# The channel layer in blocks of 512 tokens that run across batches, with its second product turned round

## The chip, the core and the metric

The kernel runs on one core of one Trainium2 chip. A core has a matrix engine (TensorE, PE in the profile, with its weight loads shown apart as PEld), a vector engine (VectorE, DVE), a scalar engine (ScalarE, ACT), a general engine (GpSimd, POOL) and a sync engine (SP) that mainly issues transfers. Each engine takes its instructions in the order in which the program lists them, and semaphores order the engines among each other. SBUF is the working memory and PSUM the memory that matmuls accumulate into; both have 128 partitions. The metric is the device time of one execution in microseconds; lower is better.

## What is computed

The program is a chain of three models on 4 batches of 768 tokens: a recurrent attention, a gated layer, and a token-and-channel mixer. The change touches only the last layer of the mixer, the channel layer. In the reference it is the last two lines of this function (B=4, 768 tokens, 384 features, 1536 hidden features):

```python
def _moe2_ref(x, w_tok1, w_tok2, w_ch1, w_ch2):
    xt = x.transpose(0, 2, 1)
    h = np.maximum(xt @ w_tok1, 0.0) @ w_tok2
    u = x + h.transpose(0, 2, 1)
    h2 = np.maximum(u @ w_ch1, 0.0) @ w_ch2
    return u + h2
```

## The kernel before

**Numbers.** A float32 value that goes into a matmul is split in two values of a shorter format: `hi`, and `lo`, which is the value less `hi`. A product of two such pairs is three matmuls into one sum (`mm3`, L521 to L524): hi by hi, hi by lo, lo by hi. So a line L522, L523 or L524 in the profile is one of those three, whatever layer it belongs to; the layer is read from the tile names behind the arrow. The first operand of `nc.tensor.matmul` behind the output is the one that is held in the array (loaded by a weight load of 128x128), and the second is streamed through it; its columns are the columns of the output.

**The channel layer.** `chan(b,hf,need)` (L632) handles half a batch, 384 tokens, at a time, so there are 8 calls. `L.UT` holds the features of one batch by its 768 tokens, as hi and lo, in the buffer GU. For each of 12 chunks f of 128 hidden features:

- the first product (L638 to L640) gives a tile of 128 hidden features by 384 tokens: 3 chunks of input features, three matmuls each, so 9 matmuls of 384 columns; the weights C1 (in the buffer SB) are held, UT streams
- `evR` (L612) takes the result out of PSUM: ACT makes `hh`, the positive part (L613), and DVE makes `hlo`, what is left of it (L614)
- one chunk later, the second product (L646, L647): for each of 3 groups of 128 tokens, `hh` and `hlo` are held and the weights C2A (buffer VHt) or, for chunks 8 to 11, C2B (buffer SW) stream with 384 output features. That makes 9 more matmuls of 384 columns, into three accumulators `acc` that stay in PSUM over all 12 chunks.

At the end three DVE additions put the accumulators onto the input `xn` (L651), which has tokens on partitions like them, and three transfers of 192 KB on SP's queue write the result (L652).

**Transposes.** Before the first call for a batch, `trans(b,L.UT)` (L541) turns the whole batch round: 18 TensorE transposes of 128x128 (L546), three to a PSUM bank, and six evictions `evT` (L538, L539), each an ACT copy to hi and a DVE subtraction to lo. No other PE work is listed between them and the matmuls around them.

**Order of the work around it.** The Python generators write out the order. `bank()` hands out five PSUM banks in turn, and three more are the accumulators. `push` emits an eviction right behind its matmuls. While the layer starts, its weights are still being read and converted: `chl` (L707) is a generator of steps, each of which loads 128x256 pieces of 64-bit input (L434), rebuilds float32 on DVE (L446 to L451) and splits it, hi on ACT (L422) and lo on POOL (L423). `both(a,b,n)` (L665) advances it by n steps for each `yield` of the layer (`n[0]`, `n[1]`, `n[2]` are 0.5, 0.2 and 0.7), and `need(k)` forces as many steps as a chunk needs before it can be emitted. The layer before, `tok2` (L626), ends with additions onto `xn` (L601).

Of the kernel before, what the change touches and what calls it, by code (L numbers as in the profile page):

```python
# [6 lines left out]
F32=mybir.dt.float32; F32R=mybir.dt.float32r; I32=mybir.dt.int32; I64=mybir.dt.int64; BF16=mybir.dt.bfloat16  # L7
# [404 lines left out]
def _dense(tc,I,O,xn,cfg):  # L412

    nc=cfg.get('wrap',lambda x:x)(tc.nc)
    THR=2.0**(0x70-127)*1.125
    A0=1.0/0.044715; CG=0.7978845608028654*0.044715
    me=_Dense(); es=ExitStack(); esT=ExitStack(); esS=ExitStack()
    R=lambda t:t.bitcast(F32)
    def split(src,hi,lo,w,p=False):

        if p: nc.gpsimd.tensor_copy(hi,src)
        else: nc.scalar.copy(hi,src)  # L422
        (nc.gpsimd if w else nc.vector).tensor_tensor(lo,src,R(hi),ALU.subtract)  # L423
    def load(src,hi,lo,parts,step=256,pool=None,ahead=2,g=1,out=None,lag=1):
# [30 lines left out]
        for i in range(0,n+lag*g,g):  # L455
            for j in range(max(i-lag*g,0),min(i-lag*g+g,n)):
                r=slice(todo[j][1],todo[j][1]+step)
                if out is None: split(Fs[j],hi[:,r],lo[:,r],True)
                else:
                    w=[pool.tile([128,step],F32R,name=n_,bufs=2) for n_ in ('sh','sl')]  # L460
                    split(Fs[j],w[0],w[1],True,True)
                    for x,y in zip(out(r),w): nc.gpsimd.dma_start(x,R(y))
            if i<n:
# [7 lines left out]
    def start(scr):  # L471
# [3 lines left out]
        psB=[es.enter_context(tc.tile_pool(name="psD",bufs=2,space=PS,side="right"))]  # L475
# [3 lines left out]
        idt=PW.tile([128,128],F32,name="idt")  # L479
# [12 lines left out]
        def bank():  # L492
            nb[0]+=1
            return psB[order[0][nb[0]%len(order[0])]].tile([128,512],F32,name="ps")

        hl=lambda t,o,n:(t[:,o:o+n],t[:,o+n:o+2*n])
# [4 lines left out]
        C2A=[a.rearrange("p (f e) -> p f e",e=384) for a in hl(VHt,0,3072)]  # L501
        XT=[X[:,i] for i in range(2)]
        XN=[X[:,i].rearrange("p k t -> p (k t)").rearrange("p (s e) -> p s e",e=384) for i in range(2)]
        L=_Dense()
# [11 lines left out]
        def late2():  # L516
            GU=es.enter_context(tc.tile_pool(name="pg",bufs=1)).tile([128,6144],F32R,name="GU")
            L.GT=[a.rearrange("p (d t) -> p d t",t=768) for a in hl(GU,0,3072)]
            L.UT=[a.rearrange("p (k t) -> p k t",t=768) for a in hl(GU,0,2304)]
            L.H1=[a.rearrange("p (k e) -> p k e",e=384) for a in hl(GU,4608,768)]  # L520
        def mm3(ps,L,Rr,first,last):  # L521
            nc.tensor.matmul(ps,L[0],Rr[0],start=first,stop=False)  # L522
            nc.tensor.matmul(ps,L[0],Rr[1],start=False,stop=False)  # L523
            nc.tensor.matmul(ps,L[1],Rr[0],start=False,stop=last)  # L524
# [4 lines left out]
        def push(it):  # L529

            few=len(order[0])==2
            if few: tick()
            more=next(it,0)!=0
            if not few: tick()
            if more: live.append(it)
        def drain():
            while live: tick()
        def evT(ps,hi,lo):  # L538
            nc.scalar.copy(hi,ps); nc.vector.tensor_tensor(lo,ps,R(hi),ALU.subtract)  # L539
            yield 1  # L540
        def trans(b,dst):  # L541
            for k in range(3):
                for hf in range(2):
                    ps=bank()[:,0:384]
                    for i in range(3):
                        nc.tensor.transpose(ps[:,128*i:128*i+128],xn[b][:,3*hf+i,128*k:128*k+128],idt)  # L546
                    push(evT(ps,dst[0][:,k,384*hf:384*hf+384],dst[1][:,k,384*hf:384*hf+384]))
                    yield 1
# [51 lines left out]
        def evX(ps,b,s):  # L600
            nc.vector.tensor_tensor(xn[b][:,s],xn[b][:,s],ps,ALU.add)  # L601
            yield 1
# [9 lines left out]
        def evR(ps,hi,lo):  # L612
            nc.scalar.activation(hi,ps,AF.Relu)  # L613
            nc.vector.scalar_tensor_tensor(lo,ps,0.0,R(hi),op0=ALU.max,op1=ALU.subtract)  # L614
            yield 1
# [10 lines left out]
        def tok2(b):  # L626
            for s in range(6):
# [1 line left out]
                for k in range(2):  # L629
                    mm3(ps,[w[:,k,128*s:128*s+128] for w in TK2],[h[:,k,:] for h in L.H1],k==0,k==1)  # L630
                push(evX(ps,b,s)); yield 1
        def chan(b,hf,need):  # L632
            acc=[psB[2].tile([128,512],F32,name="ps")[:,:384] for _ in range(3)]
            hd=[None]*12
            for f in range(13):
                if f<12:
                    need(2*(f//4)+1)
                    ps=bank()[:,:384]  # L638
                    for k in range(3):
                        mm3(ps,[w[:,k,128*f:128*f+128] for w in L.C1],[x[:,k,384*hf:384*hf+384] for x in L.UT],k==0,k==2)  # L640
                    hi=ph[0].tile([128,384],F32R,name="hh"); lo=ph[0].tile([128,384],F32R,name="hlo")
                    push(evR(ps,hi,lo)); hd[f]=(hi,lo)
                    yield 1
                if f>0:
                    need(2*((f-1)//4)+2)
                    for i in range(3):  # L646
                        mm3(acc[i],[h[:,128*i:128*i+128] for h in hd[f-1]],[w[:,f-1,:] for w in C2A] if f<9 else [w[:,f-9,:] for w in L.C2B],f==1,f==12)  # L647
                    yield 1
            for i in range(3):
                s=3*hf+i  # L650
                nc.vector.tensor_tensor(xn[b][:,s],xn[b][:,s],acc[i],ALU.add)  # L651
                nc.sync.dma_start(O[:,6*b+s],xn[b][:,s])  # L652
            tick()
        def go(*its):

            its=[i for i in its if i is not None]
            while its:
                for it in list(its):
                    if next(it,0)==0: its.remove(it)
        def seq(*its):  # L660
            for it in its:
                for _ in it: yield 1
        f=lambda a:a.rearrange("p a b -> p (a b)")
        lw=lambda nm,W,parts,**k:load(I[nm],f(W[0]),f(W[1]),parts,**k)
        def both(a,b,n=1):  # L665
            t=0.0
            for _ in a:
                t+=n
                while t>=1: next(b,0); t-=1
                yield 1  # L670
        def pre():
            for h in (1,0):
                for i in range(2):
                    nc.sync.dma_start(R(WIN[i])[:,:,512*h:512*h+512],scr[i].rearrange("p (k f) -> p k f",f=1024)[:,:,512*h:512*h+512])
            yield from trans(0,XT)
            yield from V(0)
            yield from U(0)
        def rest():
            late()
            lo_=lw('wo',L.WO,[(0,1536,0)])  # L680
            with tc.tile_pool(name="px",bufs=1) as PX:
                w=PX.tile([128,4608],F32,name="wsg")
                for i in range(3): nc.sync.dma_start(w[:,1536*i:1536*i+1536],I['wsg'][:,1536*i:1536*i+1536])
                def sg():
                    for i in range(12):
                        r=slice(384*i,384*i+384)
                        split(w[:,r],f(L.WSG[0])[:,r],f(L.WSG[1])[:,r],i%2==0)
                        yield 1
                ld=seq(sg(),lo_)
                go(both(me.gen,ld)); go(both(trans(1,XT),ld)); go(ld)  # L690
            late2()
            for b in range(4):
                if b==3: ld=seq(lw('tok1',TK1,[(0,1536,0)]),lw('tok2',TK2,[(0,1536,0)])); xsplit(0); go(both(Sg(b),ld,2)); go(ld)
                else: go(Sg(b)); go(V(b+1))
                if b<3:
                    go(Out(b)); go(U(b+1))
                    if b<2: go(trans(b+2,XT))
            hold=[]
            go(tok1(0,hold)); go(Out(3))
            drain(); tokr(hold[0]); drain()  # L700
            esT.close(); esS.close()
            order[0]=[0,0,1,1,1]
            with tc.tile_pool(name="ph",bufs=3,side="right") as PH_, tc.tile_pool(name="px2",bufs=2,side="right") as PX:
                ph[0]=PH_
                k=dict(pool=PX,ahead=2,g=2)
                at=[0]
                def chl():  # L707
                    for q in range(0,6,2):
                        yield from lw('ch1',L.C1,[(1536*i+256*q,1536*i+256*q+512,1536*i+256*q) for i in range(3)],**k)
                        at[0]+=1  # L710
                        w=(C2A,768*q) if q<4 else (L.C2B,768*q-3072)
                        yield from lw('ch2',w[0],[(768*q,768*q+1536,w[1])],**k)
                        at[0]+=1
                ld=chl()
                def need(n):
                    while at[0]<n: next(ld,0)
                n=cfg.get('nl',(.3,.4,.5))
                for b in range(4):
                    if b<3: xsplit(b+1)
                    go(both(tok2(b),ld,n[0]))  # L720
                    if b<3: go(both(tok1(b+1),ld,n[1]))
                go(both(trans(0,L.UT),ld,n[1]))
                for b in range(4):
                    go(both(chan(b,0,need),ld,n[2])); go(both(chan(b,1,need),ld))
                    if b<3: go(trans(b+1,L.UT))
                drain()
            es.close()
        me.gen=pre(); me.rest=rest
# [18 lines left out]

    return {k:v.view(np.int64) if v.dtype==np.float64 else v for k,v in r.items()}
def unpack(o):
    return np.ascontiguousarray(o.reshape(2,2,32,24,384)[:,::-1].reshape(128,24,384).transpose(1,0,2)).reshape(4,768,384)  # L750

def _jobs(cfg):

# [52 lines left out]
```

## Time and profile before

| | |
|---|---|
| median of 3 runs | 995.02 us (994.36 to 1000.47) |
| the profiled execution, its own time | 995.25 us |
| its span on the engines | 993.5 us |
| TensorE clock granted, mean | 0.931 |
| instructions | 23135 |

The span runs from the first instruction to the last; 1.75 us of the profiled execution's time lie around it. The page of a profile gives for each engine its busy time, and for groups of equal instructions their count, their mean duration and the engine's idle time just before them together with the engine that ended it. The view by windows gives the busy times in chosen stretches; the timeline lists single instructions with start and duration. A matmul's duration in the timeline is longer than the distance to the next one, since matmuls overlap in the pipeline: what counts for a stream of them is the distance from start to start.

### The profile page before, as it was taken

How to read it: one execution, taken by the hardware profiler on the slowest of the kernel's cores; microseconds unless marked ns; L12 is line 12 of the kernel's file. 1: busy time of each engine (PE TensorE's matmuls, PEld its weight loads, DVE VectorE, ACT ScalarE, POOL GpSimd, SP SyncE). 2: the span in 40 equal slices, each digit the busy share in tenths (PEclk: the TensorE clock that was granted, in tenths of full speed). 3: DMA queues.
4: the chain of work that ended last, by engine and by line, in shares of the span. 5: the costliest groups of instructions: out<-in, count | busy, mean ns of one | idle time of the engine just before them, and what ended most of it. 6: DMA issues, size and time to landing. Idle time of an engine off the chain costs nothing.

```text
span 993.5 us, 23135 instructions
## 1 busy us (share of the span) xinstructions
PE 864.2 (87%) x9643; PEld 821.1 (83%) x9644; DVE 607.7 (61%) x1246; ACT 378.1 (38%) x857; POOL 352.9 (36%) x456
## 2 busy tenths in 40 slices
PE   5357486778789899999999997979899999999998
PEld 4157476767777689999999996879799999999998
DVE  7969967989921777965848897878613123123122
ACT  2035365747587663343423432524312112112111
POOL 9133365999744435323333444743300000000000
PEclk8769597959799999999999998989999999999999
DMA  8651556776455032000000021322200000000000
GB/s 192 149 127 32 133 137 152 199 196 166 100 99 177 2 129 63 1 1 1 1 1 1 12 82 46 107 82 93 83 1 24 1 24 24 1 25 24 1 24 24
DMA packets 60024, 68.05 MB, mean 68 GB/s; under 512 B 30224, under 2 KB 37136, under 8 KB 59920
## 3 DMA queue, kind: packets, MB, share of 16 engines
q1 hardware_dynamic: 57808, 60.28, 23.1%
q0 software_dynamic: 2112, 6.29, 2.0%
q8 instruction: 76, 1.25, 0.5%
q14 instruction: 28, 0.23, 0.1%
HBM read 51.61 MB, written 7.86 MB: 60 GB/s over the span
## 4 chain that ended last, share of the span: by engine, by line
PE 67%; DVE 12%; DMA 7%; ACT 5%; POOL 4%; issue 3%; SPq 2%; ACTq 0%; DVEq 0%; POOLq 0%
PE ps L522 18%; PE ps L523 18%; PE ps L524 18%; PE gm L131 2%; DMA aq<-in_qt_dram 2%; DMA kq<-in_kq_dram 2%; DVE F L446 2%; DVE F L447 2%; PE yp L278 1%; PE gm L249 1%; PE ps L546 1%; DVE F L448 1%; DMA md<-gf 1%; PE gm L156 1%; PE wm L331 1%
## 5 line engine op out<-in xcount | busy, mean ns | idle before, releaser
L614 DVE SCALAR_TENSOR_TENSOR hlo<-ps,hh 128x384 fp32r<-128x384 f32 x96 | 53.5, 557 | 207.5 <-ACT hh L613 207.5
L613 ACT ACTIVATE hh<-ps 128x384 fp32r<-128x384 f32 x96 | 47.2, 491 | 228.4 <-PE ps L524 228.4
L522 PE MATMUL ps<-GU,SB 128*128 128x384 f32 x288 | 98.3, 341 | 0.0
L524 PE MATMUL ps<-GU,SB 128*128 128x384 f32 x288 | 98.1, 341 | 0.0
L523 PE MATMUL ps<-GU,SB 128*128 128x384 f32 x288 | 97.7, 339 | 0.0
L206 DVE TENSOR_TENSOR p<-Li,T 128x31 f32<-128x31 f32 (+13 forms) x186 | 75.1, 419 | 3.6
L208 DVE TENSOR_TENSOR T<-T,p 128x31 f32<-128x31 f32 (+13 forms) x186 | 74.4, 416 | 3.4
L131 PE MATMUL gm<-aq,kq 128*64 128x64 f32 x768 | 42.6, 276 | 36.8 <-DMA kq<-in_kq_dram 31.7
L131 PEld LDWEIGHTS gm<-aq,kq 128*64 128x64 f32 x768 | 38.4, 187 | 39.1 <-issue 26.3
L523 PE MATMUL ps<-SB,VHt 128*128 128x384 f32 x192 | 65.6, 342 | 2.3 <-POOL SB L423 2.3
L524 PE MATMUL ps<-VHt,hlo 128*128 128x384 f32 x192 | 65.3, 340 | 1.3 <-DVE hlo L614 1.3
L522 PE MATMUL ps<-SB,VHt 128*128 128x384 f32 x192 | 65.7, 342 | 0.0
L524 PE MATMUL ps<-SB,VHt 128*128 128x384 f32 x192 | 65.1, 339 | 0.0
L522 PE MATMUL ps<-VHt,hh 128*128 128x384 f32 x192 | 64.9, 338 | 0.0
L523 PE MATMUL ps<-VHt,hh 128*128 128x384 f32 x192 | 64.6, 337 | 0.0
L142 POOL TENSOR_SCALAR_AFFINE_SELECT aq<-aq 32x512 f32<-32x512 f32 x48 | 36.7, 765 | 76.2 <-ACT aq L139 69.6
L270 POOL TENSOR_TENSOR yr<-v,nn 64x192 f32<-64x192 f32 x96 | 58.6, 610 | 13.4 <-DMA v<-in_vn_dram 4.1
L589 POOL TENSOR_TENSOR q<-q,u 128x384 f32<-128x384 f32 x32 | 36.9, 1157 | 66.6 <-DVE q L588 66.6
L522 PE MATMUL ps<-X,SA 128*128 128x384 f32 x144 | 50.6, 351 | 5.7 <-DVE xn L601 3.1
L522 PEld LDWEIGHTS ps<-GU,SB 128*128 128x128 f32 x288 | 54.6, 190 | 0.6 <-DVE GU L539 0.5
L523 PEld LDWEIGHTS ps<-GU,SB 128*128 128x128 f32 x288 | 54.5, 189 | 0.6 <-DVE GU L539 0.6
L524 PEld LDWEIGHTS ps<-GU,SB 128*128 128x128 f32 x288 | 54.4, 189 | 0.3 <-POOL SB L423 0.3
(159 smaller groups left out, 2357.3 us busy)
## 6 DMA issues: line engine op xcount, KB each, us to landing
kq<-in_kq_dram SPq DMA_DIRECT2D x48, 256.0 KB, 4.7
st<-in_ch_dram SPq DMA_DIRECT2D x36, 256.0 KB, 2.8
aq<-in_qt_dram SPq DMA_DIRECT2D x12, 512.0 KB, 6.6
v<-in_vn_dram SPq DMA_DIRECT2D x12, 384.0 KB, 4.9
kn<-in_kn_dram SPq DMA_DIRECT2D x12, 384.0 KB, 9.1
out_dram<-xn SPq DMA_DIRECT2D x24, 192.0 KB, 1.9
tw<-td SPq DMA_DIRECT2D x24, 128.0 KB, 4.4
st<-in_win_dram POOLq DMA_DIRECT2D x12, 256.0 KB, 5.6
```

The costliest lines, as they stand in the source:

```text
L131: nc.tensor.matmul(gp[T_[par],n,:],kq[F_,par,64*n:64*n+64],aq[F_,par,n//2,n%2,:],start=True,stop=True)
L142: if blk==0: nc.gpsimd.affine_select(out=a,in_=a,pattern=[[0,8],[-64,2],[1,32]],compare_op=ALU.is_gt,fill=0.0,base=0,channel_multiplier=-1)
L206: nc.vector.tensor_tensor(p,Li[:,j,j+1:].unsqueeze(1).to_broadcast([128,w,n]),T[:,:w,j].unsqueeze(2).to_broadcast([128,w,n]),ALU.mult)
L208: nc.vector.tensor_tensor(T[:,:w,j+1:],T[:,:w,j+1:],p,ALU.add)
L270: n0=8*h+cc; nc.gpsimd.tensor_tensor(YRs[bb][gc%3][T_[par],:,par,:],VS[bb][T_[par],n0:n0+7:2,:],NNs[g%3][T_[par],16*bb+n0:16*bb+n0+7:2].un ...
L446: for j in m: nc.vector.tensor_scalar(F[j],w[j][:,:,1],3,0x3FFFFFF8,ALU.logical_shift_left,ALU.bitwise_and)
L522: nc.tensor.matmul(ps,L[0],Rr[0],start=first,stop=False)
L523: nc.tensor.matmul(ps,L[0],Rr[1],start=False,stop=False)
L524: nc.tensor.matmul(ps,L[1],Rr[0],start=False,stop=last)
L589: nc.gpsimd.tensor_tensor(gt,gt,u2[:,d,t],ALU.mult)
L613: nc.scalar.activation(hi,ps,AF.Relu)
L614: nc.vector.scalar_tensor_tensor(lo,ps,0.0,R(hi),op0=ALU.max,op1=ALU.subtract)
```

## The change

The layer now works on six blocks of 512 tokens. A block is four groups of 128 tokens counted through all batches (`divmod(4*i+j,6)`), so two of the blocks hold tokens of two batches. Its input, turned round, has two buffers `L.UB` in GU instead of the one `L.UT`, each of 3 chunks by 512 tokens, hi and lo.

The first product is the same with 512 columns instead of 384. In the second product the operands change places: a 128x128 piece of C2A or C2B is held, and `hh` and `hlo` stream with 512 tokens, so the three accumulators are three groups of 128 output features by 512 tokens. The result thus has features on partitions. The input is added to it in that layout too, from the hi and lo of `UB`, in two DVE additions into a tile `o` (a pool of two buffers) that is written in one transfer of 256 KB. This is emitted for each accumulator right after its last matmul. The host's `unpack` puts the axes in order.

The transposes of the next block (`tblk`, three banks of four transposes, three evictions) are emitted within the block before it: one bank's worth after each of the chunks f=6, 7 and 8. The first block's are emitted ahead of the layer.

```diff
+    OT=O.rearrange("p a b -> p (a b)").rearrange("p (e t) -> p e t",t=3072)
...
-            L.UT=[a.rearrange("p (k t) -> p k t",t=768) for a in hl(GU,0,2304)]
+            L.UB=[[a.rearrange("p (k t) -> p k t",t=512) for a in hl(GU,3072*i,1536)] for i in range(2)]
...
-        def chan(b,hf,need):
-            acc=[psB[2].tile([128,512],F32,name="ps")[:,:384] for _ in range(3)]
-            hd=[None]*12
+        def tblk(i):
+            for k in range(3):
+                ps=bank()
+                for j in range(4):
+                    b,n=divmod(4*i+j,6)
+                    nc.tensor.transpose(ps[:,128*j:128*j+128],xn[b][:,n,128*k:128*k+128],idt)
+                push(evT(ps,L.UB[i%2][0][:,k],L.UB[i%2][1][:,k]))
+                yield 1
+        def chan(i,need,nxt):
+            acc=[psB[2].tile([128,512],F32,name="ps") for _ in range(3)]
+            ut=L.UB[i%2]; hd=[None]*12
+            def out(e):
+                o=ph[0].tile([128,512],F32,name="o",bufs=2)
+                nc.vector.tensor_tensor(o,acc[e],R(ut[0][:,e]),ALU.add)
+                nc.vector.tensor_tensor(o,o,R(ut[1][:,e]),ALU.add)
+                nc.sync.dma_start(OT[:,e,512*i:512*i+512],o)
             for f in range(13):
                 if f<12:
                     need(2*(f//4)+1)
-                    ps=bank()[:,:384]
+                    ps=bank()
                     for k in range(3):
-                        mm3(ps,[w[:,k,128*f:128*f+128] for w in L.C1],[x[:,k,384*hf:384*hf+384] for x in L.UT],k==0,k==2)
-                    hi=ph[0].tile([128,384],F32R,name="hh"); lo=ph[0].tile([128,384],F32R,name="hlo")
+                        mm3(ps,[w[:,k,128*f:128*f+128] for w in L.C1],[x[:,k] for x in ut],k==0,k==2)
+                    hi=ph[0].tile([128,512],F32R,name="hh"); lo=ph[0].tile([128,512],F32R,name="hlo")
                     push(evR(ps,hi,lo)); hd[f]=(hi,lo)
                     yield 1
                 if f>0:
                     need(2*((f-1)//4)+2)
-                    for i in range(3):
-                        mm3(acc[i],[h[:,128*i:128*i+128] for h in hd[f-1]],[w[:,f-1,:] for w in C2A] if f<9 else [w[:,f-9,:] for w in L.C2B],f==1,f==12)
+                    for e in range(3):
+                        w=[w[:,f-1,128*e:128*e+128] for w in C2A] if f<9 else [w[:,f-9,128*e:128*e+128] for w in L.C2B]
+                        mm3(acc[e],w,hd[f-1],f==1,f==12)
+                        if f==12: out(e)
                     yield 1
-            for i in range(3):
-                s=3*hf+i
-                nc.vector.tensor_tensor(xn[b][:,s],xn[b][:,s],acc[i],ALU.add)
-                nc.sync.dma_start(O[:,6*b+s],xn[b][:,s])
+                if f>5: next(nxt,0)
             tick()
...
-                go(both(trans(0,L.UT),ld,n[1]))
-                for b in range(4):
-                    go(both(chan(b,0,need),ld,n[2])); go(both(chan(b,1,need),ld))
-                    if b<3: go(trans(b+1,L.UT))
+                go(both(tblk(0),ld,n[1]))
+                for i in range(6):
+                    go(both(chan(i,need,tblk(i+1) if i<5 else iter(())),ld,n[2]))
```

More of the change, by code (lines that the diff above doesn't have):

```diff
@@ L749, in unpack @@
 def unpack(o):
-    return np.ascontiguousarray(o.reshape(2,2,32,24,384)[:,::-1].reshape(128,24,384).transpose(1,0,2)).reshape(4,768,384)
+    y=o.reshape(128,3,48,2,32)[:,:,:,::-1].reshape(128,3,4,768)
+    return np.ascontiguousarray(y.transpose(2,3,1,0)).reshape(4,768,384)
 def _jobs(cfg):
```

## The prediction

> **What bounds the kernel now.** I read the page first, then the busy times by stage, then the timeline at the joints of the channel layer, and last the waits. On the page, the chain of work that ended last is mostly PE. The windows cut the span where the channel layer starts (666.7), where its first call ends (717.1) and where its last matmul ends (989.9).
>
> ```profile
> span 993.5 us, 23135 instructions
> ...
> PE 67%; DVE 12%; DMA 7%; ACT 5%; POOL 4%; issue 3%; SPq 2%; ACTq 0%; DVEq 0%; POOLq 0%
> ```
>
> ```profile
> core 0: us, PE busy (x) PEld busy (x) DVE busy (x) ACT busy (x) POOL busy (x), PEclk, DMA share, GB/s
> ...
> 666.70:717.10 50.40, 43.60 (x236) 41.26 (x235) 40.08 (x102) 20.85 (x57) 21.58 (x21) 0.97 0.27 90
> 717.10:989.90 272.80, 272.80 (x1566) 271.01 (x1565) 66.64 (x124) 48.51 (x102) 0.00 (x0) 1.00 0.05 16
> 989.90:993.50 3.60, 0.00 (x0) 0.00 (x0) 0.59 (x2) 0.00 (x0) 0.00 (x0) 1.00 0.46 164
> ```
>
> So in seven of the eight calls PE never rests, at clock 1.00, and DVE is busy 66.64 of 272.80 us: only PE's own time counts there. In the first call PE rests for 6.8 us. Nothing ahead of 666.7 is touched.
>
> **The change, part by part.** The number of streamed columns stays: 8 x 12 x 18 = 1728 matmuls of 384 columns become 6 x 12 x 18 = 1296 of 512. What can be gained is what a matmul costs apart from its columns, so I compare the distance from start to start in dense streams, 18 matmuls of 384 columns here and 35 of 512 in an earlier layer, both at full clock:
>
> ```profile
> 830.04 0.34 PE L522 MATMUL ps<-SW,hh 128*128 128x384 f32 x1
> ...
> 832.99 0.34 PE L524 MATMUL ps<-SW,hlo 128*128 128x384 f32 x1
> 833.16 2.20 PE L546 MATMUL ps<-idt,xn 128*128 128x128 f32 x18
> 835.28 0.45 PE L522 MATMUL ps<-GU,SB 128*128 128x384 f32 x1
> ...
> 838.69 0.34 PE L522 MATMUL ps<-VHt,hh 128*128 128x384 f32 x1
> ```
>
> ```profile
> 522.14 0.39 PE L522 MATMUL ps<-SA,X 128*128 128x512 f32 x1
> ...
> 529.85 0.39 PE L523 MATMUL ps<-SA,X 128*128 128x512 f32 x1
> ```
>
> 2.95/17 = 173.5 ns for 384 columns and 7.71/34 = 226.8 ns for 512. The 128 more columns cost 53.3 ns, 0.416 ns each, so 13.8 ns of either is fixed. The Trainium skill, TensorE: Matmul & The Clock Gate, section Back-to-back issue gap, gives an isolated warm matmul N/2.4 + 2.5 ns; by its fixed part the 432 matmuls fewer would save an estimated 1.1 us. Its 162.5 ns for N=384 is not what the trace shows (173.5), so the rows decide.
>
> *Steady step.* The fence also gives the price of a turn between batches. Matmul 832.99 is the last of one call and 838.69 the 19th of the next: 5.70 us, where 19 steps of 175.7 ns (below) would take 3.34, so a turn costs 2.36. Three turns are 7.1 of the 272.80; the rest over 7 x 12 chunks is 3.163 us a chunk. 18 x 173.5 is 3.123, so 0.04 a chunk is small hesitation. After: 18 x 226.8 + 0.04 = 4.122. 96 x 3.163 = 303.6 becomes 72 x 4.122 = 296.8: **-6.9** (432 x 13.8 ns, and 24 x 0.04). Bounds: 0 if the step just grows with the columns, -9.7 if the hesitation goes as well.
>
> *Transposes within a block.* What a turn costs besides its 18 transposes is seen beside the same 18 where nothing waits for them:
>
> ```profile
> 431.01 2.13 PE L546 MATMUL ps<-idt,xn 128*128 128x128 f32 x18
> 432.89 0.42 PE L522 MATMUL ps<-SB,VHt 128*128 128x384 f32 x1
> 433.15 0.34 PE L523 MATMUL ps<-SB,VHt 128*128 128x384 f32 x1
> ```
>
> 18 in 1.88 us are 0.104 each, and the first matmul behind them takes 0.26 instead of 0.17. A turn thus hides little: 2.36 is 1.97 of work and 0.4 of waiting. After, 60 transposes stand in 15 groups of four: 4 x 0.104 + 0.09 = 0.51, 7.6 in all, against 7.1: **+0.6** rounded. The batches are no longer a multiple of the block, so six transposes leave the exposed start and join them, and every group pays its own 0.09. Bounds: -0.8 without that, +6 if each group waits 0.4 as a turn does. Their evictions (0.6 on ACT, 0.7 on DVE, rows below) lie beside a half chunk of 2.06 us.
>
> *The start.* The first transposes wait for a PSUM bank:
>
> ```profile
> 666.70 1.15 PE L546 MATMUL ps<-idt,xn 128*128 128x128 f32 x9
> 669.58 1.69 PE L546 MATMUL ps<-idt,xn 128*128 128x128 f32 x9 [1.73 <-DVE xn L601]
> 670.99 0.69 PE L522 MATMUL ps<-GU,SB 128*128 128x384 f32 x1
> 671.47 0.52 PE L523 MATMUL ps<-GU,SB 128*128 128x384 f32 x1
> 671.79 0.52 PE L524 MATMUL ps<-GU,SB 128*128 128x384 f32 x1
> ```
>
> ```profile
> 668.97 1.02 DVE L601 TENSOR_TENSOR xn<-xn,ps 128x384 f32<-128x384 f32 x2
> 669.41 2.38 ACT L539 CAST GU<-ps 128x384 fp32r<-128x384 f32 x6
> 669.91 2.88 DVE L539 TENSOR_TENSOR GU<-ps,GU 128x384 fp32r<-128x384 f32 x6
> ```
>
> The fourth bank is held by an addition L601 that stands behind weight conversion on DVE. The new start needs three banks, so all 12 transposes run at once; but their evictions stand behind the same L601 on DVE, which ends at 669.99. The first lo is there at 669.99 + 0.68 = 670.7, and the first matmul can go a little before it: **-0.4** against 670.99. The slow steps of 0.32 behind the pause stay, since the stretch without matmuls is about as long. Bounds: 0, and -1.9 if the slow steps (ten, 0.15 too long each) go too.
>
> *Stalls in the first block.* These are PE's waits in the first window:
>
> ```profile
> PE ps L523 <- POOL SW L423: 2.5, 2, 1.7
> PE ps L546 <- DVE xn L601: 1.7, 1, 1.7
> PE ps L524 <- DVE hlo L614: 1.3, 1, 1.3
> PE ps L522 <- ACT SW L422: 1.2, 1, 1.2
> ```
>
> Without the second line it is 5.0, and 5.8 with 0.2 of restart for each of the four. They come from conversion steps in the queues of DVE, ACT and POOL. The pacing gives one step less ahead of the layer (0.2 x 3 yields instead of 0.2 x 6), so each comes a yield or two later; the need at f=8 forces the missing one, and at f=9 both versions stand at the same step and force the last three. But PE spends 4.12 on a chunk instead of 3.16, so the three conversion steps around f=1 to f=3 (some 2.7 us each) fit: the wait for hlo goes. At f=9 I follow the queues from T, the end of f=8's first product (700.0):
>
> ```profile
> 700.00 0.49 ACT L613 ACTIVATE hh<-ps 128x384 fp32r<-128x384 f32 x1 [0.62 <-PE ps L524]
> ...
> 703.57 0.70 ACT L422 CAST SW<-F 128x256 fp32r<-128x256 f32 x2
> ```
>
> ```profile
> 702.74 0.76 DVE L451 SCALAR_TENSOR_TENSOR F<-sq,F 128x256 f32<-128x256 f32 x2
> ...
> 706.91 0.75 DVE L451 SCALAR_TENSOR_TENSOR F<-sq,F 128x256 f32<-128x256 f32 x2
> ```
>
> ```profile
> 704.04 1.46 POOL L423 TENSOR_TENSOR SW<-F,SW 128x256 fp32r<-128x256 f32 x2 [3.88 <-ACT SW L422]
> 707.84 4.91 POOL L423 TENSOR_TENSOR SW<-F,SW 128x256 fp32r<-128x256 f32 x4 [2.34 <-ACT SW L422]
> ```
>
> After, f=9's first product ends at T+4.1, ACT's hh behind it at T+4.8, and only then ACT splits the first piece of C2B, T+5.2: PE waits 1.1. The lo of that piece comes from POOL at T+6.1: 0.4 more. The next two pieces leave DVE at about T+8.6 (behind hlo, 3.1 us as from 704.2 to 707.66), and POOL, slowed beside a busy DVE, took until 3.0 after that: T+11.7, where PE arrives at T+10.7: 1.0. Together 2.6 instead of 5.8: **-3.2**. Bounds: -5.8 and 0.
>
> *The end, and the turn from block to block.* Rows for additions, evictions and transfers:
>
> ```profile
> 988.89 1.60 DVE L651 TENSOR_TENSOR xn<-xn,ps 128x384 f32<-128x384 f32 x3 [1.00 <-PE ps L524]
> ```
>
> ```profile
> L553 DVE SCALAR_TENSOR_TENSOR q<-q,ps 128x512 f32<-128x512 f32 x24 | 16.3, 681 | 8.4 <-ACT q L552 8.4
> ...
> L552 ACT ACTIVATE q<-ps 128x512 f32<-128x512 f32 x24 | 14.3, 598 | 31.1 <-PE ps L524 17.4 <-POOL VHt L423 13.5
> ```
>
> ```profile
> st<-in_ch_dram SPq DMA_DIRECT2D x36, 256.0 KB, 2.8
> ...
> out_dram<-xn SPq DMA_DIRECT2D x24, 192.0 KB, 1.9
> ```
>
> Before, DVE keeps up with the accumulators: the last addition ends 0.59 after PE (989.90), and 3.0 for the transfer and the program's end follow. After, each accumulator takes two additions of 0.68 (I take L553's time for both), 1.36, but PE finishes one every 0.68. The first starts at P-1.36 (P is PE's end), ends at P, and its transfer lands about 2.0 later (between 1.9 and 2.8). The third needs that tile of `o`, which has two buffers: it starts at P+2.05 and ends at P+3.4. The tail is 3.4 + 3.0 + 0.1 = 6.5 instead of 3.6: **+2.9**. Bounds +0.8 (DVE keeps pace) and +3.8 (a landing of 2.8).
>
> The same queue stands at the five turns: `hlo` of the next block's f=0 waits on DVE behind the third output until P+3.4, ends at P+4.1, and is wanted by PE at P+4.35 (two half chunks of 2.06, one matmul of 0.23). I cost it at nothing; the cover is 0.25 us, and with a landing of 2.8 each turn would lose about 0.6, 3 in all. The accumulators are free by P+2.8. SP has nothing but these transfers by then.
>
> **Sum.** -6.9 + 0.6 - 0.4 - 3.2 + 2.9 = -7.0 against the profiled execution's own 995.25 us (0.2 above the median): **988.3 us**. A measurement of this kernel can tell about 1% from no change, so this is within 1%.
>
> **Rivals.**
>
> 1. *More of it goes.* The 0.04 a chunk falls away and the conversion is done in time because PE asks later: -9.7 and -5.8 in place of -6.9 and -3.2 gives 982.9. For it: the stream into SW at 830.04 shows no hesitation. Against it: three conversion steps are still forced at f=9.
> 2. *The step grows with the columns.* Then 72 x 4.217 is again 303.6, and the time is 995.2. Against it: 226.8 ns is less than 4/3 of 173.5 (231.3), and 173.5 is far more than the columns' own 160. For it: the 512 rows are from another buffer. (The fixed part in the Trainium skill, TensorE: Matmul & The Clock Gate, would put the time at an estimated 993, on the same side.)
> 3. *The queue at the turn is late.* Landing at 2.8 and later costs 3 to 5 us over the five turns: 991 to 993.
> 4. *Slower.* The transposed block is written into GU while matmuls read the other half of GU. If they waited for these writes, each of the 15 evictions would show whole: 0.6 + 0.68 + 0.2 of hand-over, 1.5 us, 22 in all, and 1010. It decides beyond 1% from 1.1 us each. Against it: at 670.99 matmuls read GU while DVE is writing other parts of it until 672.79.
>
> That the transposes are hidden by moving them is no gain in my sum: PE does them anyway.
>
> **How the numbers follow.** My forecast, with its bounds 985 to 992, has 0.50; rival 1 0.24, rival 2 0.13, rival 3 0.07, rival 4 0.06. Rival 1 and a corner of the forecast lie more than 1% below, so faster is 0.25, slower is 0.07 (rival 4 and something unseen), and within 1% is 0.68. The range leaves out rival 4 and the far end of rival 1: 980 to 996.
>
> **What would show it.** Matmuls of 512 columns 0.227 apart, a chunk of 4.12 us in the later blocks; transposes in groups of four with some 0.5 us from the matmul before to the one behind; first-block waits of 2 to 3 us, all for SW; a DVE wait for a landing of `o` ahead of the third output, and 6.5 us from the last matmul to the end. It is wrong if the chunk is 4.2, if PE idles at the turns, or if PE waits for GU within a block.

## The result, and the profile after

| | kernel before | changed kernel |
|---|---|---|
| median, 22 runs each | 998.07 us | 992.16 us |
| ratio, 95% interval | | 0.9945, [0.9926, 0.9963] |
| profiled execution, its span | 995.25, 993.5 us | 988.68, 987.0 us |
| channel layer: first transposes to the end | 666.70 to 993.5: 326.8 us | 664.62 to 987.0: 322.4 us |

The change makes the kernel 0.55% faster, 5.5 us with an interval of 3.7 to 7.4. In the profiled executions the span is 6.5 us shorter, of which 2.1 lie ahead of the layer, where no instruction changed: this start of the layer falls anywhere between 662.0 and 672.2 us in the profiles below. So the layer is compared by itself: 4.4 us shorter. (One execution of c_turn_transposes, 1035 us at a granted clock of 0.84, and one of h_pace_start, 1223 us at 0.64, are left out of all that follows.)

The windows of the changed kernel, cut where the layer begins, where its first block ends and where its last matmul ends:

```profile
core 0: us, PE busy (x) PEld busy (x) DVE busy (x) ACT busy (x) POOL busy (x), PEclk, DMA share, GB/s
...
664.60:724.90 60.30, 56.20 (x251) 44.43 (x249) 43.12 (x104) 22.77 (x57) 21.56 (x21) 1.00 0.25 80
724.90:980.40 255.50, 253.50 (x1120) 205.16 (x1118) 68.25 (x101) 42.92 (x72) 0.00 (x0) 1.00 0.04 15
980.40:987.00 6.60, 0.00 (x0) 0.00 (x0) 2.71 (x5) 0.00 (x0) 0.00 (x0) 0.85 0.32 119
```

In the first block PE rests 4.1 us instead of 6.8. In the later blocks, where it never rested before, it now rests 2.0. And the end takes 6.6 us instead of 3.6. PE's waits in the layer are:

```profile
PE ps L525 <- DVE hlo L616: 2.0, 1, 2.0
PE ps L524 <- DVE xn L603: 1.9, 1, 1.9
PE ps L524 <- ACT SW L423: 1.0, 1, 1.0
PE ps L526 <- POOL SW L424: 0.8, 1, 0.8
```

The wait for hlo in the first call is gone and those for SW have shrunk from 3.7 to 1.8 (the second is at the start). The 2.0 for hlo is new: the timelines of PE and DVE show it at the turn from the second block to the third.

```profile
778.33 0.40 PE L524 MATMUL ps<-hh,VHt 128*128 128x512 f32 x1
780.69 0.50 PE L525 MATMUL ps<-hlo,VHt 128*128 128x512 f32 x1 [1.96 <-DVE hlo L616]
```

```profile
774.35 0.68 DVE L649 TENSOR_TENSOR o<-ps,GU 128x512 f32<-128x512 f32 x1
775.07 0.69 DVE L650 TENSOR_TENSOR o<-o,GU 128x512 f32<-128x512 f32 x1
778.62 0.69 DVE L649 TENSOR_TENSOR o<-ps,GU 128x512 f32<-128x512 f32 x1 [2.86 <-DMA out_dram<-o]
779.35 0.69 DVE L650 TENSOR_TENSOR o<-o,GU 128x512 f32<-128x512 f32 x1
779.95 1.28 DVE L616 SCALAR_TENSOR_TENSOR hlo<-ps,hh 128x512 fp32r<-128x512 f32 x2
```

DVE reaches the third output at 775.8 and stands until the transfer of the first has landed; the next block's hlo is listed behind it. DVE waits for a landing in this way at the end of each of the six blocks, 0.8 us at the other five. The view of line L651 gives the time to landing:

```profile
DMA to landing us min/median/max: 2.0/2.0/4.1
```

A landing of 4.1 us comes once (why is not known) and costs PE 2.2 us at that turn; at the other four, by the starts of its half chunks, it loses 0.16 to 0.25. The last block ends in the same way. PE's last matmul ends at 980.36, and DVE's last output comes 3.6 us later:

```profile
982.56 0.69 DVE L649 TENSOR_TENSOR o<-ps,GU 128x512 f32<-128x512 f32 x1 [0.81 <-DMA out_dram<-o]
983.29 0.69 DVE L650 TENSOR_TENSOR o<-o,GU 128x512 f32<-128x512 f32 x1
```

The steady step, in starts of matmuls two chunks apart, then of a half that holds weights in SW, and around a group of transposes:

```profile
838.09 0.39 PE L524 MATMUL ps<-GU,SB 128*128 128x512 f32 x1
...
846.38 0.39 PE L524 MATMUL ps<-GU,SB 128*128 128x512 f32 x1
```

```profile
815.01 0.40 PE L524 MATMUL ps<-hh,SW 128*128 128x512 f32 x1
...
817.11 0.40 PE L524 MATMUL ps<-GU,SB 128*128 128x512 f32 x1
```

```profile
854.44 0.39 PE L526 MATMUL ps<-hh,VHt 128*128 128x512 f32 x1
854.67 0.60 PE L640 MATMUL ps<-idt,xn 128*128 128x128 f32 x4
855.03 0.47 PE L524 MATMUL ps<-GU,SB 128*128 128x512 f32 x1
855.34 0.39 PE L525 MATMUL ps<-GU,SB 128*128 128x512 f32 x1
```

Two chunks take 8.29 us, so a step is 230.3 ns, not 226.8, and the nine on SW take 2.10, 233.3 each. A group of transposes takes 0.36 and makes the next step 0.08 longer; by the half chunks around it, it costs 0.42 in all.

At the start, PE's first matmul follows 3.34 us behind the first transposes, and only the first two steps are long:

```profile
664.62 1.47 PE L640 MATMUL ps<-idt,xn 128*128 128x128 f32 x12
667.96 0.49 PE L524 MATMUL ps<-GU,SB 128*128 128x512 f32 x1 [1.86 <-DVE xn L603]
668.68 0.50 PE L525 MATMUL ps<-GU,SB 128*128 128x512 f32 x1 [0.23 <-DVE GU L541]
669.02 0.39 PE L526 MATMUL ps<-GU,SB 128*128 128x512 f32 x1
669.25 0.40 PE L524 MATMUL ps<-GU,SB 128*128 128x512 f32 x1
```

The first matmul needs only the hi of the first eviction; the second needs its lo and waits for it. From then on the steps are 0.23, at full clock.

### The profile page after: what moved, and what is told of

Read it like the earlier page. It is cut to its first block, busy times and chain, and to the rows that moved or that the text cites. A ratio compares the mean times of both kernels' runs of the same rounds, so it can differ in the third digit from the quotient of the medians.

```text
span 987.0 us, 22208 instructions
## 1 busy us (share of the span) xinstructions
PE 858.2 (87%) x9212; PEld 758.7 (77%) x9212; DVE 613.4 (62%) x1228; ACT 374.5 (38%) x827; POOL 352.6 (36%) x456
## 4 chain that ended last, share of the span: by engine, by line
PE 63%; DVE 17%; DMA 7%; ACT 6%; issue 4%; SPq 2%; POOL 2%; DVEq 0%; ACTq 0%; POOLq 0%
PE ps L525 18%; PE ps L524 18%; PE ps L526 18%; DVE T L208 2%; DVE p L206 2%; DVE F L447 2%; DMA aq<-in_qt_dram 2%; PE gm L131 2%; DVE F L448 2%; PE gm L249 2%; PE yp L278 1%; DMA kq<-in_kq_dram 1%; DMA md<-gf 1%; DVE F L449 1%; DMA tw<-td 1%
## 5 line engine op out<-in xcount | busy, mean ns | idle before, releaser
L616 DVE SCALAR_TENSOR_TENSOR hlo<-ps,hh 128x512 fp32r<-128x512 f32 x72 | 49.7, 691 | 167.4 <-ACT hh L615 167.4
L615 ACT ACTIVATE hh<-ps 128x512 fp32r<-128x512 f32 x72 | 43.0, 598 | 214.6 <-PE ps L526 214.6
L524 PE MATMUL ps<-GU,SB 128*128 128x512 f32 x216 | 86.3, 399 | 1.9 <-DVE xn L603 1.9
L525 PE MATMUL ps<-GU,SB 128*128 128x512 f32 x216 | 84.8, 392 | 0.2 <-DVE GU L541 0.2
L526 PE MATMUL ps<-GU,SB 128*128 128x512 f32 x216 | 84.8, 392 | 0.2 <-POOL SB L424 0.2
L525 PE MATMUL ps<-hlo,VHt 128*128 128x512 f32 x144 | 56.5, 392 | 2.0 <-DVE hlo L616 2.0
L526 PE MATMUL ps<-hh,VHt 128*128 128x512 f32 x144 | 56.7, 393 | 0.0
L524 PE MATMUL ps<-hh,VHt 128*128 128x512 f32 x144 | 56.6, 393 | 0.0
L524 PE MATMUL ps<-X,SA 128*128 128x384 f32 x144 | 48.8, 339 | 5.6 <-DVE xn L603 3.2
L156 PE MATMUL gm<-kq 128*64 128x64 f32 x768 | 34.6, 258 | 18.9 <-issue 7.1
L524 PEld LDWEIGHTS ps<-GU,SB 128*128 128x128 f32 x216 | 40.6, 188 | 10.7 <-ACT GU L541 2.1
L526 PE MATMUL ps<-X,SA 128*128 128x384 f32 x144 | 48.3, 335 | 0.0
```

The lines of the kernel that those rows point to most:

```text
L156: nc.tensor.matmul(gp[T_[par],n],c_,c_,start=True,stop=True)
```

## The experiments

In all of them PE's half chunks are read from the starts in the timeline, and the layer from its first transposes to the end, as above. The times of one table row are from one chip and one set of runs of the kernel before.

| kernel | median us | ratio to before, 95% | layer, us |
|---|---|---|---|
| a_o4 | 987.65 | 0.9926 [0.9901, 0.9950] | 318.4 |
| b_pool_sum | 986.73 | 0.9914 [0.9883, 0.9944] | 316.5 |
| c_turn_transposes | 1012.46 | 1.0154 [1.0103, 1.0206] | 341.7 |
| d_turned_384 | 1000.22 | 1.0064 [1.0039, 1.0088] | 333.2 |
| e_held_in_x (one run) | 985.51 | | 315.7 |
| f_stream_moved (one run) | 992.22 | | 318.3 |
| g_pace | 983.07 | 0.9869 [0.9830, 0.9908] | 314.7 |
| h_pace_start | 982.60 | 0.9884 [0.9845, 0.9923] | not read |
| i_before_pace | 997.22 | 1.0025 [1.0002, 1.0047] | 327.7 |
| j_pace_x | 981.16 | 0.9853 [0.9821, 0.9885] | 313.7 |
| k_pace_start_x | 980.42 | 0.9849 [0.9822, 0.9875] | 313.1 |

Many of these intervals overlap with each other or with the changed kernel's: a_o4, for one, is 1.9 us below the changed kernel by the ratios, which is not clear of noise, and 4.0 by the layer. Where a few microseconds decide, the reading rests on one profiled execution of each kernel and on the waits in it. In these, half chunks of one kind that wait for nothing agree within some 0.02 us, but the clock behind the pause at the start makes up to 1.5 us by chance (below).

**Who holds up the turn and the end: a_o4 and b_pool_sum.**

```diff
-                o=ph[0].tile([128,512],F32,name="o",bufs=2)
+                o=ob[e]   # a, b: ob = three of four slices of xn[0], in turn
...
-                nc.vector.tensor_tensor(o,acc[e],R(ut[0][:,e]),ALU.add)
-                nc.vector.tensor_tensor(o,o,R(ut[1][:,e]),ALU.add)
+                nc.vector.tensor_tensor(o,o,acc[e],ALU.add)   # b
...
+                if f==10:   # b
+                    for e in range(3): nc.gpsimd.tensor_tensor(ob[e],R(ut[0][:,e]),R(ut[1][:,e]),ALU.add)
```

> The changed kernel with the output tile o taken from a ring of four slices of xn[0] (its batch has been turned round by then) instead of a pool of two, so that no output waits for a transfer to land; still two additions for each accumulator. Theory: the waits at the turns (3.1 us in the changed kernel's profile, one of them 2.2) and a part of the tail come from DVE standing behind the landing of o, with hlo of the next block queued behind it. Expected: from PE's end to the end 5.7 us instead of 6.6 (six additions in a row), waits for hlo at the turns gone, together about 4 us less than the changed kernel. Rival: the turns wait for the additions themselves; then only the 0.9 of the tail goes.

> As the first run, and POOL adds the hi and lo of the input into the output tile ahead (behind chunk f=10), so that DVE has one addition for each accumulator, as before the change. Theory: DVE's 0.69 then keeps pace with PE's 0.69 for an accumulator; the last addition ends 0.7 after PE instead of 3.6, so the tail is 3.8 us instead of 6.6, and the turns do not wait: about 6 us less than the changed kernel. Rival: POOL's additions slow DVE or come late (in the first block POOL is still splitting weights), and some of this is lost again.

The layer is 4.0 us shorter than the changed kernel's with a_o4 and 5.9 with b_pool_sum. In both no half chunk at a turn is long any more, and PE has no wait for hlo there. The last additions on DVE, of a_o4 (the second of two for each accumulator in L651) and of b_pool_sum:

```profile
982.51 0.68 DVE L650 TENSOR_TENSOR xn<-ps,GU 128x512 f32<-128x512 f32 x1
983.23 0.69 DVE L651 TENSOR_TENSOR xn<-xn,GU 128x512 f32<-128x512 f32 x1
```

```profile
982.51 2.08 DVE L650 TENSOR_TENSOR xn<-xn,ps 128x512 f32<-128x512 f32 x3 [1.55 <-PE ps L526]
```

PE's last matmul starts at 980.81 and 983.41 and takes 0.39, so DVE ends 2.7 and 0.8 us after PE, where the changed kernel's ends 3.6 after. POOL's additions cost PE nothing, in the first block either. So the landing of o is the turns' wait and 0.9 of the tail; the second addition is the other 2 us of the tail. The rivals fall.

**Where the transposes stand: c_turn_transposes.**

```diff
                         if f==12: out(e)
                     yield 1
-                if f>5: next(nxt,0)
+            for _ in nxt: pass
```

> The changed kernel with the three groups of transposes of the next block emitted at the turn, behind the last matmul of a block, as before the change, instead of behind f=6, 7 and 8. Theory: within a block the transposes hide nothing of PE's own work, but at the turn their evictions would stand on DVE behind the six additions: the first product of the next block would end about 6.3 us after PE's last matmul instead of 2.1, less 1.3 for the transposes that no longer stand in the block and less the 0.6 that the turn waits now: +2.3 us a turn, 11 to 12 us slower than the changed kernel. Rival: a turn costs its transposes and 0.4 as before the change, and the waits for hlo go: about 1 us faster.

19.3 us more in the layer, more than the 11 to 12. At the third turn, from its timeline:

```profile
837.09 1.47 PE L640 MATMUL ps<-idt,xn 128*128 128x128 f32 x12
...
838.36 0.50 PE L524 MATMUL ps<-GU,SB 128*128 128x512 f32 x1
...
840.78 1.88 DVE L541 TENSOR_TENSOR GU<-ps,GU 128x512 fp32r<-128x512 f32 x3
841.52 0.50 PE L525 MATMUL ps<-GU,SB 128*128 128x512 f32 x1 [2.66 <-DVE GU L541]
```

The evictions stand behind the six additions (L541 starts at 840.78), as expected. By the starts of the half chunks the first three turns cost 4.3 to 4.6 us each with their transposes, where the changed kernel pays 1.9 for a turn and a block's groups: 2.5 more, near the 2.3. Most of the rest is the clock. After the fourth turn, with a pause that is no longer, the steps are almost twice as long, as the timeline shows and then the windows:

```profile
895.63 0.80 PE L525 MATMUL ps<-GU,SB 128*128 128x512 f32 x1 [2.64 <-DVE GU L541]
...
897.08 0.63 PE L525 MATMUL ps<-GU,SB 128*128 128x512 f32 x1
897.51 0.63 PE L526 MATMUL ps<-GU,SB 128*128 128x512 f32 x1
```

```profile
890.00:960.00 70.00, 64.66 (x272) 52.08 (x272) 21.40 (x32) 11.49 (x20) 0.00 (x0) 0.93 0.06 23
```

Steps of 0.43 make the last two turns 5.2 and 4.0 dearer than the changed kernel's, and the layer's start is 1.5 dearer in the same way. In the stretch around the fourth turn alone, 889 to 905, the granted clock is 0.79; around the third, 835 to 845, it is 1.00. About 13 of the 19.3 us are thus the evictions' place (2.5 at each of five turns), some 6 the clock, and the rest longer stalls in the first block. So standing within a block is worth much, though it hides none of PE's own work: what it avoids is an eviction behind the outputs.

**The turned product without the wide block: d_turned_384.**

```diff
-                    for i in range(3):
-                        mm3(acc[i],[h[:,128*i:128*i+128] for h in hd[f-1]],[w[:,f-1,:] for w in C2A] if f<9 else [w[:,f-9,:] for w in L.C2B],f==1,f==12)
+                    for e in range(3):
+                        w=[w[:,f-1,128*e:128*e+128] for w in C2A] if f<9 else [w[:,f-9,128*e:128*e+128] for w in L.C2B]
+                        mm3(acc[e],w,hd[f-1],f==1,f==12)
+                        if f==12: out(e)
```

(`out` as in the change, with 384 tokens and three tiles.)

> The kernel before with only the second product turned round (weights held, hh and hlo of 384 tokens stream, output features on partitions, two additions into three output tiles); half batches of 384 and the transposes between batches stay. Theory: turning by itself changes no distance between matmuls, a chunk stays at 3.16 us; what the change gains in the step is all from 512 columns. The two additions make the tail 1.6 longer and the evictions at the three batch turns 1.3 later each: about 5.5 us slower than the kernel before. Rival: holding the weights is itself dearer (in the changed kernel a half chunk on buffer SW takes 2.10 against 2.04 by 226.8 ns): then halves on SW take 1.62 instead of 1.56 here, 2 us more.

6.4 us more in the layer than the kernel before (5.5 expected; the other 0.9 is mostly longer stalls in the first call), and 1.0064 by the runs. The halves stay at 1.58, 1.59 and, on SW, 1.56 us. So turning the product by itself makes no step longer or shorter; it only adds the additions. What it does is to let the second product stream 512 tokens, where it could only stream its 384 output features before. All of the gain in the step comes from 512 columns, and the longer steps on SW appear only with them.

**The step that came out 3.5 ns longer: e_held_in_x and f_stream_moved.**

```diff
-            L.C2B=[a.rearrange("p (f e) -> p f e",e=384) for a in hl(SW,0,1536)]
+            L.C2B=[a.rearrange("p (f e) -> p f e",e=384) for a in hl(X.rearrange("p a k t -> p (a k t)"),0,1536)]   # e
...
-                    hi=ph[0].tile([128,512],F32R,name="hh"); lo=ph[0].tile([128,512],F32R,name="hlo")
+                    hi=ph[0].tile([128,544],F32R,name="hh")[:,:512]; lo=ph[0].tile([128,544],F32R,name="hlo")[:,:512]   # f
```

> b_pool_sum with the second half of the second product's weights (C2B) in the buffer X instead of SW; X is free by then and held matmul operands at 226.8 ns a step in an earlier layer. It asks why a step of 512 columns takes 233.3 ns where C2B is held and 230.4 elsewhere in the layer, where 226.8 was predicted. Theory 1 (the place of the held operand): nine matmuls with C2B held take 2.04 to 2.07 us instead of 2.10. Theory 2 (the streamed operand hh, hlo, or its width): they stay at 2.10.

> b_pool_sum with the tiles hh and hlo 544 columns apart instead of 512, so that the streamed operand of the second product lies at other addresses. Theory 1 (place of the held operand): nothing changes, 2.07 and 2.10 us for nine matmuls. Theory 2 (place of the streamed operand): the halves of the second product change, towards 2.04, while those of the first stay at 2.07.

Held from X, nine matmuls take 2.06 to 2.07 us (229.1 ns a step, a mean over 21 halves); with hh and hlo moved, 2.10 as before (233.2). So the place of the held weights makes the excess on SW, and that of the streamed tile does not; the halves on VHt even became 1 ns a step longer with it (231.0 against 229.9). It does not get to 2.04: in the kernels here mean steps of 225 to 227 ns and of 233 to 237 stand side by side at fixed places among the nine matmuls, and what makes them is open. The layer of f_stream_moved is 1.8 us longer mainly for another reason: its first nine steps take 4.17 us instead of 2.69, with steps of 0.43 and a granted clock of 0.76 from 675 to 682, after a pause of the same 3.3 us.

**The stalls in the first block: g_pace and i_before_pace.**

```diff
-'nl':(0.5,0.2,0.7)
+'nl':(0.5,0.2,1.0)
```

> b_pool_sum with one step of weight conversion for each yield of the layer (1.0 instead of 0.7), so that no step is forced at f=9: the last pieces are converted behind f=6. Theory: the 3.3 us of stalls in the first block (f=7, f=9, f=10) come from steps that are emitted too late; at most 0.5 is left, 2.5 to 3 us less than b_pool_sum. Rival: DVE is the bound of the first block, and the stalls only move to earlier chunks as waits for hlo.

> The kernel before with nothing but the pacing of g_pace (one step of weight conversion for each yield, 1.0 instead of 0.7). It asks whether the 3.3 us that the change took off the stalls of the first call could have been had without it. Theory: in blocks of 384 tokens PE gives DVE 38 us for some 27 us of conversion and 7 of hlo, so the stalls move to earlier chunks as waits for hlo, and 3 to 5 of 6.4 us stay: 1.5 to 3 us less than before. Rival: the pacing alone was at fault; at most 1 us stays, 5.5 us less.

In g_pace 1.2 us of stalls is left of 3.1 (3.3 in the expectation, which counts the longer step behind transposes in; half chunks 0.23 and 1.0 longer, now for hlo), and the layer is 1.8 us shorter than that of b_pool_sum: part of what the theory asked (at most 0.5 left, 2.5 to 3 gained), with the rival's waits for hlo as the rest. The same pacing in the kernel before does no good: the waits are now of another kind,

```profile
PE ps L522 <- ACT hh L613: 4.0, 3, 1.6
PE ps L546 <- DVE xn L601: 1.7, 1, 1.7
PE ps L524 <- DVE hlo L614: 1.6, 2, 0.8
```

and by the half chunks 8.6 us are lost where it was 6.4; the ratio of 1.0025 says the same. More stays than the theory allowed (3 to 5), and nothing of the rival is left. So the stalls that the change took away were not there for the taking by this pacing: with 384 tokens PE asks too soon for what ACT and DVE can deliver. Turning the product does not take them away either (7.6 us by the half chunks of d_turned_384), so it is the longer chunk that gives room.

**The pause at the start, and what is left together: h_pace_start, j_pace_x, k_pace_start_x.**

```diff
-                    go(both(tok2(b),ld,n[0]))
+                    go(both(tok2(b),ld,n[0] if b<3 else 0.0))   # h and k
```

> g_pace without conversion steps during the token layer's last product ahead of the layer. Theory: the pause from the first transposes to the first matmul (3.3 us) is the wait for additions that stand behind conversions on DVE; without them it falls to about 2, and the slow step behind it goes: 1.5 us less than g_pace. The two conversions move into the first block, where DVE has room (26 of 40 us busy): at most 1 us of stalls comes back. Rival: the first block is then too full and stalls by 3 us or more.

> g_pace with C2B held from X as in e_held_in_x (nine matmuls 2.07 instead of 2.10 there, 24 times): 0.7 us less than g_pace in the profile, less than a measurement of the time can tell.

> j_pace_x without conversion steps during the token layer's last product, as h_pace_start, whose profiled execution cannot be read for this. Theory as there: the pause from the first transposes to the first matmul falls from 3.3 to about 2 us, the slow first steps (0.6 us) go, and at most 1 us of stalls comes back in the first block: 1 to 1.5 us less than j_pace_x. Rival: the first block is too full and stalls by 3 us or more.

For h_pace_start only its time can be told, which is not apart from g_pace. j_pace_x does what was expected (the layer 1.0 us shorter than g_pace, where 0.7 was asked). In k_pace_start_x the pause is

```profile
668.29 1.47 PE L640 MATMUL ps<-idt,xn 128*128 128x128 f32 x12
669.57 0.50 PE L524 MATMUL ps<-GU,SB 128*128 128x512 f32 x1
670.29 0.50 PE L525 MATMUL ps<-GU,SB 128*128 128x512 f32 x1 [0.22 <-DVE GU L541]
```

1.28 us instead of 3.33, more than expected; but 1.5 us more stalls come back in the first block (2.7 instead of 1.2), so the layer gains 0.6 and not 1 to 1.5. The first nine steps take as long as before. The theory had their 0.6 us for a slow clock, but it is the second matmul's wait for the lo of the first eviction, which stands in both kernels (0.22 here, and 0.72 from the first start to the second). j_pace_x and k_pace_start_x are faster than both kernels of the case: 0.985 of the kernel before, with intervals that end below 0.9926, where the changed kernel's begins.

## Why the prediction was right

The forecast of 988.3 us, 7.0 below the profiled execution, was within 1% and a little faster, and so it came out: 4.4 us in the layer, 5.5 by the runs. That the changed kernel's profiled execution took 988.68 us, so near the forecast, is luck: 2.1 of its 6.5 us lie ahead of the layer, where nothing changed. The terms, against the half chunks of the two profiles:

| step | predicted, us | measured, us | from |
|---|---|---|---|
| steady step | -6.9 | -4.4 | 48 chunks of 4.147 and 24 (with SW) of 4.175 against 96 of 3.163 |
| transposes within a block | +0.6 | -0.8 | 15 groups at 0.42 against three turns of 2.36 |
| start | -0.4 | -1.8 | pause 3.34 against 4.29; the first nine steps 0.6 longer than later ones against 1.5 |
| stalls, first block | -3.2 | -3.3 | 3.1 against 6.4 by half chunks, transposes taken out |
| turns from block to block | 0 | +3.0 | 2.2, and four of 0.16 to 0.25 |
| end | +2.9 | +3.0 | 6.6 against 3.6 |

They add to -4.3 of the measured -4.4.

Of the prediction's own signs, those for the stalls, the transposes and the end came or nearly came (a wait for a landing ahead of the third output, 6.6 us where 6.5 was named). One sign of being wrong came too: PE idles at the turns. The chunk, 4.15 to 4.18, lies between the 4.12 that was forecast and the 4.2 that would have refuted it.

- *Right, and shown.* That the step gains from 512 columns; d_turned_384 leaves nothing of it to the turning. The end: the buffers of `o` and the second addition are its two parts, 0.9 and 2 (a_o4, b_pool_sum). The stalls: one for hlo gone, the waits for SW smaller, and bound to the longer chunk (i_before_pace, d_turned_384). Rival 4 did not come: no wait for GU within a block, and none is seen in the waits but 0.2 at the start.
- *Mis-sized: the steady step.* The distance for 512 columns was taken from an earlier layer, 226.8 ns; here it is 230.3, and 233.3 on SW. Before the change it is the other way round: the 173.5 ns came from SW, the fastest halves of that layer, and the others step 176 ns, which the prediction booked as hesitation. A single stream was taken for the mean twice. The sentence for rival 2, that "the 512 rows are from another buffer", named the weak point: by e_held_in_x the place of the held operand does count, though for 4 ns of 233. The sum had 229.0 ns a step (4.122 a chunk) and the mean is 230.9, which makes 2.5 us over 1296 matmuls. Rival 2, no gain in the step at all, was thus about a third right. Rival 1 did not come: neither the step nor the stalls gave as much as it asked (9.7 and 5.8).
- *Mis-sized: the turn.* It was costed "at nothing; the cover is 0.25 us", and the same lines and rival 3 put late landings at 3 us and more. Measured is 3.0: 2.2 from one landing of 4.1, and 0.8 at the four others, where the cover was to hold. A cover that small is no cover; rival 3 should have been in the sum.
- *Mis-sized: the start.* The first matmul was expected a little before the lo of the first eviction; it needs only the hi, and came some 0.5 us sooner. That the slow steps stay "since the stretch without matmuls is about as long" did not come: in the changed kernel only a wait for that lo is left. After 3.3 us of pause the first nine steps took 2.69 in most profiles here, but 4.17 in f_stream_moved and in c_turn_transposes; after 4.3 us they were slow in the kernel before and in d_turned_384, and not in i_before_pace. So this term is partly chance. The Trainium skill, TensorE: Matmul & The Clock Gate, Part 1, says that the clock is set by an activity window of about 3.4 us that runs freely. By that, equal pauses may end differently; these runs agree.
- *Mis-sized: the transposes.* They cost 0.42 a group, not 0.51, so moving them gained a little instead of losing a little.

Two terms came out dearer than the sum had them (steady step 2.5, turns 3.0) and two cheaper (transposes and start, 1.4 each), and they partly cancelled. That the layer's gain lies within 3 us of the forecast owes something to this.

## What to carry to other kernels

When an eviction turns from one instruction to two, compare it with the time in which PE makes the next accumulator: at 1.36 us against 0.69 it falls behind, and everything listed behind it on that engine, the next block's first eviction above all, inherits the delay. An output tile that waits for a landing puts every landing into a compute queue, here also the one of 4.1 us beside a median of 2.0; more buffers took the waits at the turns away, and an idle engine that prepared the sum took away most of the tail. And a move that hides no work can still be worth its place: with the transposes at the turn instead of inside the block the same kernel lost 19 us, about 13 of them without the clock.

## What the runs showed of the hardware that was not expected

Here a matmul's distance depended on where its held operand lies: with the same streamed tiles, 233.4 ns a step (a mean over 21 halves) when C2B was held from SW and 229.1 when from X (512 columns), while with 384 columns, in d_turned_384, the halves that hold it from SW were the shortest of the layer (1.56 us against 1.58 and 1.59). The same idle time before the second matmul at the third and at the fourth turn of c_turn_transposes (2.66 and 2.64 us) left the clock full once and halved once (steps of 0.23 and 0.43).
